# Attention with a mixture of depths on one core: gate products and first ranking later, one transpose per group's sums

## The chip, the core and the metric

The kernel runs on one core of one Trainium2 chip. The core has a matrix engine (TensorE: PE for its matmuls, PEld for its weight loads), a vector engine (VectorE, DVE), an activation engine (ScalarE, ACT), a general engine (GpSimd, POOL), and queues that start DMA transfers; SP is the queue that issues nearly all of them here. Each engine works through its own list of instructions in order, and semaphores tie the lists together. The time of a kernel is the device time of one execution in microseconds (us). The times given are medians over runs; every other number is read from one execution that the hardware profiler recorded.

## The reference

Two blocks follow each other. The first is attention over 8 batches, 12 heads, 448 tokens and head size 64, with root-mean-square normalized queries and keys. The second is a feed-forward net that only the 128 highest scoring tokens of each batch pass through.

```python
def rmsnorm(x, g):
    rms = np.sqrt(np.mean(x * x, axis=-1, keepdims=True) + 1e-06)
    return x / rms * g
q_n, k_n = (rmsnorm(q, g_q), rmsnorm(k, g_k))
scores = scale * np.matmul(q_n, k_n.transpose(0, 1, 3, 2))
scores = scores - np.max(scores, axis=-1, keepdims=True)
attn = np.exp(scores)
attn = attn / (np.sum(attn, axis=-1, keepdims=True) + 1e-09)
x = np.matmul(attn, v)               # then heads side by side: (8, 448, 768)

scores = np.einsum('bsd,d->bs', x, w_gate)
out = x.copy()
for b in range(B):
    top_idx = np.argpartition(-scores[b], capacity)[:capacity]   # 128 of 448
    xe = x[b, top_idx]
    h = np.maximum(xe @ w1, 0.0)     # 768 -> 1024
    ye = h @ w2                      # 1024 -> 768
    g = 1.0 / (1.0 + np.exp(-scores[b, top_idx]))
    out[b, top_idx] = x[b, top_idx] + g[:, None] * ye
```

All data are 32-bit floats.

## The kernel before, in words

**Groups, units, sections.** Four heads make a group; three groups make a batch, 24 groups (n = 0 to 23) in all. A group's 448 keys are cut into seven slices of 64, so that there are 168 units (`u`). The loop at the end of `fast` goes through sections `q` of four units. In a section it issues `scores(u)` (L284, matmuls L292, exponentials L301) for its units and, some units behind, `values(u)` (L309, matmuls L316). What else has to be done is put between them: pieces of the feed-forward net, tasks of a group that ended, and small steps by slot (one slot per unit).

**The sums of the exponentials.** `add_probs` (L324) adds the probabilities of a group's units on the vector engine (L338). For groups 0 to 5, GpSimd adds the first two units (L332) into a buffer called `tok` in the profile, and the vector engine adds that result last (L342); for groups 0 to 5 and 23 the last unit isn't added but becomes a second term. `sum_keys` (L364) sums over keys with matmuls against `pick_pair`, a matrix of ones and zeros (L372): per term four matmuls 224 wide into four different blocks of 32 output rows. A 32-bit matmul is two instructions in the profile, so a term shows as x8. ScalarE copies the result (L380), `invert_sums` (L388) transposes it with two matmuls (L397) and the vector engine takes reciprocals (L399, `rden`). The 448 tokens are four blocks of 112; two of the blocks lie in columns 0 to 111 of the result (`jj` 0) and two in columns 112 to 223 (`jj` 1), and each half takes one of the two transposes.

**From a group to tokens.** `to_tokens(n, c)` (L404) transposes half a group's output (four matmuls L415 into `x_ps`) and the vector engine multiplies it by the reciprocals (L417) into `x`, the batch's tokens.

**Gate and ranking.** `gate(n)` (L433) makes the group's share of the gate scores: four products with a sum each (L441, 112x256, and a short read of the accumulator). After the batch's third group, `spread(b)` (L451) adds the shares, `score_rows` (L463) spreads the scores over partitions with four transposes into `row_ps` (L470), `count` (L480) compares (four times L486), `annotate` (L496) makes five small steps (L501 to L505), `select` (L507) has GpSimd write the chosen rows by four indirect DMAs (L513), and `load_selected` (L529) reads them back through SP (`xe`, L531).

**The feed-forward net.** `mixture(g)` (L538) handles the chosen rows of one batch or of two in pieces: transposes (L561), first layer (L590), second layer (L609), the gated addition (L618), the indirect write to the output (L628). Batch 0 alone is mixture 0: two pieces of transposes, four of the first layer (twelve matmuls 128x128 each) and four of the second (four matmuls 128x384 each). `piece(q)` (L778) issues the next one; there are two places per section for it, and `BEGIN` (L640) and the condition in L781 and L782 say in which sections only the first place is used.

**What sets the order.** `finish` (L694) puts the tasks of a group that ended in a queue, each with the section and place from which it may run; `opening` (L652) runs one of them, with the exception that the inversion may be followed by another. `last_tokens` (L719) puts `gate`, `store_x` and `spread` into slots and `ranks_of` into the queue. `invert_sums` is queued by `sum_keys` (L384 to L386): in the same section if `long_next` (L705) says that a piece of the net follows, and otherwise at the head of the next section. `prepare` (L668) and the lines after it put the squares (L210), their sums (L219), the powers on GpSimd (L220, `rinv`), the broadcast of the norms through memory (`rows` L231, `bc` L242) and the scaling of the queries (L251, `qT`) into slots of the sections before. All this is settled when the program is built: each engine's list is fixed.

**Banks.** The matmul results lie in eight banks: four (`sc`) turn over among scores, and second halves of `x_ps`; two hold the values; one (`aux`) serves `den_ps`, `row_ps` and `x_ps`; one (`moe`) serves the net, and before the net starts it is lent out (`spare`, L125, and the choice in L391 to L395).

Of the kernel before, what the change touches and what calls it, by code (L numbers as in the profile page):

```python
# [10 lines left out]
F32 = mybir.dt.float32  # L11
# [57 lines left out]
def fast(  # L69
# [21 lines left out]
    nc = tc.nc  # L91

    B, NP, _, S = loads.src["qT"].shape
    CP = 112
    NJ = S // CP
    D = 64
    NI = S // D
    H = 2 * NP
    GH = 4
    NG = H // GH  # L100
# [7 lines left out]
    n_groups = B * NG  # L108
    scale = 1.0 / math.sqrt(D)

    const = ctx.enter_context(tc.tile_pool(name="const", bufs=1))
    norm_pool = ctx.enter_context(tc.tile_pool(name="norm", bufs=2))
# [30 lines left out]
    ident = const.tile([128, 128], F32, name="ident")  # L143
# [10 lines left out]

    gg = const.tile([128, 1], F32, name="gg")

    pick_pair = const.tile([128, 32], F32, name="pick_pair")
    nc.vector.memset(pick_pair, 0.0)
    for c in range(2):
        nc.vector.memset(pick_pair[D * c : D * (c + 1), c : c + 1], 1.0)  # L160
    nc.vector.scalar_tensor_tensor(
        out=gg, in0=loads.gcol[:, 0:1], scalar=scale, in1=loads.gcol[:, 1:2], op0=OP.mult, op1=OP.mult
    )

    ps = ps_moe.tile([128, 512], F32, tag="moe", name="warm_ps")
# [116 lines left out]
    probs, sums, avs, xTs, rdens, xs = {}, {}, {}, {}, {}, {}  # L282
# [81 lines left out]
    def sum_keys(n):  # L364

        ps = aux([128, 512], "den_ps")
        terms = [sums.pop(n)] + lasts.pop(n, [])
        for t in terms:
            for hh in range(2):
                for odd in range(2):  # L370
                    o = 64 * odd + 32 * hh
                    nc.tensor.matmul(  # L372
                        out=ps[o : o + 32, 0 : S // 2],
                        lhsT=pick_pair,
                        rhs=t[:, hh].rearrange("k (jj odd p) -> k odd jj p", odd=2, p=CP)[:, odd],
                        start=(t is terms[0]),
                        stop=(t is terms[-1]),
                    )
        den = norm_pool.tile([128, NJ // 2, CP], F32, name="den", bufs=1)
        nc.scalar.copy(out=den.rearrange("d j p -> d (j p)"), in_=ps[:, 0 : S // 2])  # L380
        dens[n] = den
        if n < n_groups - 1:

            q, place = now  # L384
            when = (q, place + 1) if place == 0 or long_next(q) else (q + 1, 0)
            tasks.insert(0, (when, lambda: invert_sums(n)))  # L386

    def invert_sums(n):  # L388
        den = dens.pop(n)
        shape = [128, NJ // 2, 128]  # L390
        if now[1] == 0 and PER * now[0] < units:  # L391
            pool, tag = (ps_moe, "moe") if before_layers(now[0]) else (ps_sc, "sc")
            ps = pool.tile(shape, F32, tag=tag, name="denT_ps")
        else:
            ps = aux(shape, "denT_ps")  # L395
        for jj in range(NJ // 2):
            nc.tensor.transpose(out=ps[:CP, jj, :], in_=den[:, jj, :], identity=ident)  # L397
        rden = norm_pool.tile([CP, NJ // 2, 4, 2], F32, name="rden")
        nc.vector.reciprocal(  # L399
            out=rden, in_=ps[:CP].rearrange("p jj (t r) -> p jj t r", r=32)[:, :, :, 0:2]  # L400
        )
        rdens[n] = rden.rearrange("p jj (odd hh) c -> p (jj odd) hh c", hh=2)

    def to_tokens(n, c):  # L404
        b = n // NG
# [231 lines left out]

    HALVES = 2
    PER = 2 * HALVES
    BEGIN = 3 * NG * NI // PER + 5  # L640
    units = n_groups * NI
    todo, tasks = {}, []

    def at(slot, fn, *args):
        todo.setdefault(slot, []).append(lambda: fn(*args))
# [58 lines left out]

    def long_next(q):  # L705

        if before_layers(q) or q in begin:
            return False
        return 2 <= pieces[0] < pieces[1]

    def before_layers(q):
        return done == 0 and ready.get(0, q + 1) > q
# [6 lines left out]
    def last_tokens(n):  # L719
        to_tokens(n, 1)  # L720
        b, g = divmod(n, NG)
        s = soon()
        at(s, gate, n)
        if g < NG - 1:
            return

        at(s + 4 if s >= 0 else s, store_x, b)
        at(s + 1, spread, b)
        q, place = now

        when = (q + 1 + place // 2, 0) if b < B - 1 else (q + 1, 1)
        tasks.insert(0, (when, lambda: ranks_of(b)))

    def ranks_of(b):
# [39 lines left out]
    def short(q):  # L774

        return pieces[0] == 1

    def piece(q):  # L778

        nonlocal moe, done  # L780
        slow = range(3, 5) if q * PER < units and pieces[1] > 10 else ()  # L781
        if half == 1 and (q in begin and pieces[0] > 2 or pieces[0] in slow):  # L782
            return False
        pieces[0] += 1
        if next(moe, moe) is not moe:
            return True
        if ready.get(done, q + 1) > q:
            return False
        moe = mixture(done)
        pieces[:] = 1, 2 + 8 * len(groups[done])  # L790
        done += 1
        next(moe)
        return True


    begin = range(BEGIN)
    pieces = [0, 0]
    waiting = list(range(units))
    moe, ready, done, q = iter(()), {}, 0, 0
    while done < len(groups) or tasks:  # L800
        now[:] = q, 0
        k = PER * q
# [552 lines left out]
```

## Time and profile before

| what | value |
|---|---|
| median of 3 runs | 523.1 us (522.91 to 523.53) |
| the profiled execution | 523.67 us |
| its span, from the first instruction to the last | 521.9 us |
| PE busy | 499.3 us, 96% of the span |
| VectorE busy | 338.0 us, 65% |
| ScalarE busy | 277.0 us, 53% |
| GpSimd busy | 198.1 us, 38% |
| data moved by DMA | 93.17 MB |

The busy shares are averages over a span with several stages. The kernel starts with loads, squares and scores; from about 102 us pieces of the net lie between the attention's matmuls; after about 447 us only the last group, the last rankings and the net are left. A wait is given as engine, line and what it waited for, with the total in us, the number of waits and the longest. In a timeline, each line has the start and length of a run of equal instructions in us; "[1.60 <-DVE sum L342]" at its end is the engine's idle time ahead of it and what ended that.

### The profile page before, as it was taken

How to read it: one execution, taken by the hardware profiler on the slowest of the kernel's cores; microseconds unless marked ns; L12 is line 12 of the kernel's file. 1: busy time of each engine (PE TensorE's matmuls, PEld its weight loads, DVE VectorE, ACT ScalarE, POOL GpSimd, SP SyncE). 2: the span in 40 equal slices, each digit the busy share in tenths (PEclk: the TensorE clock that was granted, in tenths of full speed). 3: DMA queues.
4: the chain of work that ended last, by engine and by line, in shares of the span. 5: the costliest groups of instructions: out<-in, count | busy, mean ns of one | idle time of the engine just before them, and what ended most of it. 6: DMA issues, size and time to landing. Idle time of an engine off the chain costs nothing. (4 is left out here: it accounts for less than half of the span.)

```text
span 521.9 us, 10414 instructions
## 1 busy us (share of the span) xinstructions
PE 499.3 (96%) x4133; PEld 283.1 (54%) x4133; DVE 338.0 (65%) x636; ACT 277.0 (53%) x507; POOL 198.1 (38%) x110
## 2 busy tenths in 40 slices
PE   5999898899999999999999999999999999899996
PEld 4544343365754534556654454556564464686595
DVE  4578798679867799697656775788464675440101
ACT  4887876666657667675454544764643434310010
POOL 4997768433544084435411344036110132020002
PEclk9999999999999999999999999999999999999999
DMA  8978879989864549968167373586222042031001
GB/s 298 374 239 292 292 242 334 313 233 328 274 177 131 153 142 312 261 229 261 26 201 221 107 240 111 187 264 180 80 76 68 4 148 77 1 122 47 30 32 35
DMA packets 43402, 93.17 MB, mean 179 GB/s; under 512 B 11059, under 2 KB 23348, under 8 KB 43346
## 3 DMA queue, kind: packets, MB, share of 16 engines
q1 hardware_dynamic: 39938, 86.11, 52.6%
q0 software_dynamic: 3264, 6.31, 3.4%
q8 instruction: 34, 0.56, 0.5%
q14 instruction: 22, 0.18, 0.1%
q10 hardware_dynamic: 144, 0.00, 0.0%
HBM read 74.93 MB, written 25.35 MB: 192 GB/s over the span
## 5 line engine op out<-in xcount | busy, mean ns | idle before, releaser
L301 ACT ACTIVATE p<-sc,rinv 128x448 f32<-128x448 f32 x336 | 186.5, 642 | 105.4 <-PE sc L292 79.8
L220 POOL TENSOR_TENSOR rinv<-ss,neg_half 128x14 f32<-128x14 f32 (+1 forms) x49 | 131.3, 2685 | 178.0 <-DVE ss L219 144.9
L292 PE MATMUL sc<-qT,kT 64*64 64x448 f32 x1344 | 153.2, 545 | 2.0 <-DVE x L417 1.2
L316 PE MATMUL av<-p,v 64*64 64x448 f32 x1344 | 146.8, 537 | 0.0
L338 DVE TENSOR_TENSOR sum<-sum,p 128x896 f32<-128x896 f32 x101 | 110.1, 1090 | 8.7 <-ACT p L301 2.5
L316 PEld LDWEIGHTS av<-p,v 64*64 64x64 f32 x1344 | 59.4, 133 | 67.7 <-issue 58.0
L292 PEld LDWEIGHTS sc<-qT,kT 64*64 64x64 f32 x1344 | 54.0, 132 | 70.6 <-issue 46.6
L219 DVE TENSOR_REDUCE ss<-sq 128x14 f32<-128x910 f32 (+1 forms) x49 | 52.4, 1074 | 18.7 <-ACT sq L210 18.5
L417 DVE TENSOR_TENSOR x<-x_ps,rden 112x512 f32<-112x512 f32 x48 | 32.9, 689 | 37.9 <-PE x_ps L415 34.6
L513 POOL DMA_INDIRECT selected<-x,rank x32 | 35.4, 1105 | 58.0 <-DVE x L505 50.0
L590 PE MATMUL moe_ps<-xeT,w 128*128 128x256 f32 (+1 forms) x288 | 56.0, 346 | 0.0
L609 PE MATMUL moe_ps<-w,hT 128*128 128x384 f32 x160 | 55.8, 492 | 0.0
L590 PEld LDWEIGHTS moe_ps<-xeT,w 128*128 128x128 f32 x288 | 46.2, 191 | 7.0 <-issue 2.8
L210 ACT ACTIVATE sq<-tok 128x896 f32<-128x896 f32 (+1 forms) x49 | 46.3, 952 | 6.2 <-DMA tok<-in_tok_dram 6.2
L441 DVE SCALAR_TENSOR_TENSOR prod<-x,wg 112x256 f32<-112x256 f32 x96 | 40.7, 424 | 3.1
L628 POOL DMA_INDIRECT out_dram<-xe,row x10 | 11.4, 1136 | 80.7 <-DVE xe L618 63.6
L609 PEld LDWEIGHTS moe_ps<-w,hT 128*128 128x128 f32 x160 | 28.8, 190 | 20.2 <-issue 4.3
L618 DVE SCALAR_TENSOR_TENSOR xe<-sc,xe 128x384 f32<-128x384 f32 (+1 forms) x7 | 3.9, 560 | 48.1 <-PE sc L609 48.1
L590 PE MATMUL sc<-xeT,w 128*128 128x256 f32 (+1 forms) x192 | 32.2, 328 | 0.3 <-ACT xeT L566 0.3
L609 PE MATMUL sc<-w,hT 128*128 128x384 f32 (+1 forms) x112 | 31.3, 440 | 0.0
L415 PE MATMUL x_ps<-ident,xT 128*112 128x128 f32 x192 | 28.9, 276 | 2.2 <-DVE rden L399 2.2
L590 PEld LDWEIGHTS sc<-xeT,w 128*128 128x128 f32 x192 | 28.8, 191 | 2.9 <-ACT xeT L566 0.5
(69 smaller groups left out, 316.2 us busy)
## 6 DMA issues: line engine op xcount, KB each, us to landing
tok<-in_tok_dram SPq DMA_DIRECT2D x48, 448.0 KB
qT<-in_qT_dram SPq DMA_DIRECT2D x24, 448.0 KB
kT<-in_kT_dram SPq DMA_DIRECT2D x24, 448.0 KB
v<-in_vp_dram SPq DMA_DIRECT2D x24, 448.0 KB
out_dram<-x SPq DMA_DIRECT2D x8, 1344.0 KB
bc<-rows SPq DMA_DIRECT2D x44, 224.0 KB
xe<-selected SPq DMA_DIRECT2D x8, 385.0 KB
w<-in_moe_w_dram SPq DMA_DIRECT2D x6, 512.0 KB
```

The costliest lines, as they stand in the source:

```text
L210: nc.scalar.activation(out=sq[:, h, :, 0:D], in_=t[:, h], func=AF.Square, scale=scale)
L219: nc.vector.tensor_reduce(out=ss[:, h], in_=sq[:, h], axis=AX.X, op=OP.add)
L220: nc.gpsimd.tensor_tensor(out=rinv[:, h].rearrange(flat), in0=ss[:, h].rearrange(flat), in1=neg_half.to_broadcast([128, (h.stop - h.start) ...
L292: nc.tensor.matmul(out=scs[hh][D * c : D * (c + 1), 0:S], lhsT=get("kT", n)[r, c, D * i : D * (i + 1)], rhs=get("qT", n)[r, c, :], start=True,
L301: nc.scalar.activation(out=p[:, hh], in_=scs[hh][:, 0:S], func=AF.Exp, scale=rinvs[n, 1][:, hh, i : i + 1],)
L316: nc.tensor.matmul(out=avs[n][c][D * hh : D * (hh + 1), 0:S], lhsT=get("v", n)[r, hh, i, :], rhs=probs[u][r, hh], start=(i == 0), stop=(i ...
L338: nc.vector.tensor_tensor(out=sums[n], in0=probs.pop(u - 1) if begins else sums[n], in1=probs.pop(u), op=OP.add)
L417: nc.vector.tensor_tensor(out=xs[b][:, :, col : col + 128].rearrange("p j (h d) -> p j h d", d=D), in0=ps[:CP].rearrange("p j (h d) -> p j ...
L441: nc.vector.scalar_tensor_tensor(out=prod, in0=xs[b][:, j, cols], scalar=1.0, in1=wg[:, cols], op0=OP.mult, op1=OP.mult, accum_out=gates[b ...
L513: w = nc.gpsimd.indirect_dma_start(out=t[:, :], out_offset=bass.IndirectOffsetOnAxis(ap=rank[:, j : j + 1], axis=0), in_=x[:, j, :], in_of ...
L590: nc.tensor.matmul(out=ps[:, i, :, :n], lhsT=w1[:, dc, 128 * (f0 + i) : 128 * (f0 + i + 1)], rhs=xeT[:, dc, 0:G, :n], start=(dc == 0), sto ...
L609: nc.tensor.matmul(out=ps[:n, :width], lhsT=hT[:, fc, i, :n], rhs=w2[:, fc, cols], start=(fc == 0), stop=(fc == NFC - 1),)
```

## The change

Four things are changed.

1. **One transpose per group's sums.** `pick_pair` becomes two matrices, one for each half `jj`, whose ones stand in different columns. The halves are then summed into the same 112 columns and different rows: per term eight matmuls 112 wide where there were four 224 wide. The copy of the result is 112 wide and not 224, there is one transpose and not two, and the reciprocal reads the same 16 values per partition in another order and writes them where they were before.
2. **Batch 0's gate products and ranking later.** `gate` of groups 1 and 2 goes two slots later, `spread` of batch 0 too, and `score_rows` of batch 0 may run from place 2 of its section and not place 0. With that, comparison, selection and loading of batch 0's rows move on.
3. **The last gate but one later.** `gate` of group 22 goes four slots later. At the end, that is behind the last addition of group 23's probabilities.
4. **Pieces.** `BEGIN` is 21 and not 20. The condition for using one place per section is put into a function, `single`, and `long_next` asks that function, so that where the second place stays empty, `invert_sums` goes to the head of the next section.

In the lists that are built, besides the parts named, this is what moves: mixture 0 starts one section later (its transposes behind those of group 5 and not group 4), each of its pieces is issued one place later, and the last one fills a place ahead of a `den_ps` that held none; on the vector engine the products of groups 1 and 2 stand behind the additions of groups 2 and 3, batch 0's comparisons behind group 3's reciprocal, and the additions of mixture 0 (L618) later; GpSimd has two powers (`rinv`) ahead of batch 0's selection where it had one ahead and one behind, and, later, batch 2's selection ahead of batch 0's indirect write to the output where it was behind it; SP issues the load of batch 0's rows behind a broadcast and a weight load that stood after it. The lists have as many scores, values, products and pieces as before.

```diff
--- before.py
+++ after.py
@@ -154,10 +154,12 @@
 
     gg = const.tile([128, 1], F32, name="gg")
 
-    pick_pair = const.tile([128, 32], F32, name="pick_pair")
+    pick_pair = const.tile([128, NJ // 2, 32], F32, name="pick_pair")
     nc.vector.memset(pick_pair, 0.0)
-    for c in range(2):
-        nc.vector.memset(pick_pair[D * c : D * (c + 1), c : c + 1], 1.0)
+    for jj in range(NJ // 2):
+        for c in range(2):
+            r = 2 * jj + c
+            nc.vector.memset(pick_pair[D * c : D * (c + 1), jj, r : r + 1], 1.0)
     nc.vector.scalar_tensor_tensor(
         out=gg, in0=loads.gcol[:, 0:1], scalar=scale, in1=loads.gcol[:, 1:2], op0=OP.mult, op1=OP.mult
     )
@@ -365,19 +367,21 @@
 
         ps = aux([128, 512], "den_ps")
         terms = [sums.pop(n)] + lasts.pop(n, [])
-        for t in terms:
+        steps = [(t, jj) for t in terms for jj in range(NJ // 2)]
+        for step in steps:
+            t, jj = step
             for hh in range(2):
                 for odd in range(2):
                     o = 64 * odd + 32 * hh
                     nc.tensor.matmul(
-                        out=ps[o : o + 32, 0 : S // 2],
-                        lhsT=pick_pair,
-                        rhs=t[:, hh].rearrange("k (jj odd p) -> k odd jj p", odd=2, p=CP)[:, odd],
-                        start=(t is terms[0]),
-                        stop=(t is terms[-1]),
+                        out=ps[o : o + 32, 0:CP],
+                        lhsT=pick_pair[:, jj],
+                        rhs=t[:, hh].rearrange("k (j p) -> k j p", p=CP)[:, 2 * jj + odd],
+                        start=(step is steps[0]),
+                        stop=(step is steps[-1]),
                     )
-        den = norm_pool.tile([128, NJ // 2, CP], F32, name="den", bufs=1)
-        nc.scalar.copy(out=den.rearrange("d j p -> d (j p)"), in_=ps[:, 0 : S // 2])
+        den = norm_pool.tile([128, CP], F32, name="den", bufs=1)
+        nc.scalar.copy(out=den, in_=ps[:, 0:CP])
         dens[n] = den
         if n < n_groups - 1:
 
@@ -387,19 +391,21 @@
 
     def invert_sums(n):
         den = dens.pop(n)
-        shape = [128, NJ // 2, 128]
+        shape = [128, 128]
         if now[1] == 0 and PER * now[0] < units:
             pool, tag = (ps_moe, "moe") if before_layers(now[0]) else (ps_sc, "sc")
             ps = pool.tile(shape, F32, tag=tag, name="denT_ps")
         else:
             ps = aux(shape, "denT_ps")
-        for jj in range(NJ // 2):
-            nc.tensor.transpose(out=ps[:CP, jj, :], in_=den[:, jj, :], identity=ident)
-        rden = norm_pool.tile([CP, NJ // 2, 4, 2], F32, name="rden")
+        nc.tensor.transpose(out=ps[:CP, :], in_=den, identity=ident)
+        rden = norm_pool.tile([CP, NJ // 2, 2, 2, 2], F32, name="rden")
         nc.vector.reciprocal(
-            out=rden, in_=ps[:CP].rearrange("p jj (t r) -> p jj t r", r=32)[:, :, :, 0:2]
+            out=rden.rearrange("p jj odd hh c -> p (odd hh) jj c"),
+            in_=ps[:CP].rearrange("p (t r) -> p t r", r=32)[:, :, 0:NJ].rearrange(
+                "p t (jj c) -> p t jj c", c=2
+            ),
         )
-        rdens[n] = rden.rearrange("p jj (odd hh) c -> p (jj odd) hh c", hh=2)
+        rdens[n] = rden.rearrange("p jj odd hh c -> p (jj odd) hh c")
 
     def to_tokens(n, c):
         b = n // NG
@@ -637,7 +643,7 @@
 
     HALVES = 2
     PER = 2 * HALVES
-    BEGIN = 3 * NG * NI // PER + 5
+    BEGIN = 3 * NG * NI // PER + 6
     units = n_groups * NI
     todo, tasks = {}, []
 
@@ -704,7 +710,7 @@
 
     def long_next(q):
 
-        if before_layers(q) or q in begin:
+        if before_layers(q) or single(q):
             return False
         return 2 <= pieces[0] < pieces[1]
 
@@ -720,15 +726,16 @@
         to_tokens(n, 1)
         b, g = divmod(n, NG)
         s = soon()
-        at(s, gate, n)
+        late = 2 if n in (1, NG - 1) else 4 if n == n_groups - 2 else 0
+        at(s + late, gate, n)
         if g < NG - 1:
             return
 
         at(s + 4 if s >= 0 else s, store_x, b)
-        at(s + 1, spread, b)
+        at(s + 1 + late, spread, b)
         q, place = now
 
-        when = (q + 1 + place // 2, 0) if b < B - 1 else (q + 1, 1)
+        when = (q + 1 + place // 2, late) if b < B - 1 else (q + 1, 1)
         tasks.insert(0, (when, lambda: ranks_of(b)))
 
     def ranks_of(b):
@@ -775,11 +782,16 @@
 
         return pieces[0] == 1
 
+    def single(q):
+
+        if q in begin:
+            return pieces[0] > 2
+        return PER * q < units and pieces[1] > 10 and pieces[0] in (3, 4)
+
     def piece(q):
 
         nonlocal moe, done
-        slow = range(3, 5) if q * PER < units and pieces[1] > 10 else ()
-        if half == 1 and (q in begin and pieces[0] > 2 or pieces[0] in slow):
+        if half == 1 and single(q):
             return False
         pieces[0] += 1
         if next(moe, moe) is not moe:
```

## The prediction

> **What bounds the kernel now.** I read the busy shares first, then PE's waits, then the timeline of PE and of the vector engine around each wait. PE is busy 96% of the span, so two things can shorten the kernel: less PE work, or fewer of the waits that make up the rest.
>
> ```profile
> PE 499.3 (96%) x4133; PEld 283.1 (54%) x4133; DVE 338.0 (65%) x636; ACT 277.0 (53%) x507; POOL 198.1 (38%) x110
> ...
> PE den_ps L372 <- DVE sum L342: 2.7, 2, 1.6
> PE x_ps L415 <- DVE rden L399: 2.2, 1, 2.2
> PE moe_ps L561 <- DMA xe<-selected: 2.2, 1, 2.2
> PE den_ps L372 <- DVE row L573: 1.3, 1, 1.3
> PE sc L292 <- DVE x L417: 1.2, 1, 1.2
> PE den_ps L372 <- DVE sum L338: 1.0, 1, 1.0
> PE denT_ps L397 <- ACT den L380: 1.0, 2, 0.5
> ```
>
> These seven lines are 11.6 us, nearly all of PE's waiting after its start. Next, PE's timeline where they lie.
>
> ```profile
> 57.13 0.58 PE L372 MATMUL den_ps<-sum,pick_pair 128*32 128x224 f32 x8 [1.60 <-DVE sum L342]
> ...
> 74.44 0.58 PE L372 MATMUL den_ps<-sum,pick_pair 128*32 128x224 f32 x8 [1.05 <-DVE sum L342]
> ...
> 84.57 0.65 PE L415 MATMUL x_ps<-ident,xT 128*112 128x128 f32 x4 [2.19 <-DVE rden L399]
> ...
> 101.82 0.55 PE L561 MATMUL moe_ps<-ident,xe 128*128 128x128 f32 x3 [2.17 <-DMA xe<-selected]
> ...
> 110.14 0.43 PE L397 MATMUL denT_ps<-ident,den 128*112 128x128 f32 x2
> 110.40 0.60 PE L415 MATMUL x_ps<-ident,xT 128*112 128x128 f32 x4
> 110.84 2.84 PE L590 MATMUL moe_ps<-xeT,w 128*128 128x128 f32 x24
> ```
>
> Three of the first four waits end with the vector engine, whose own list shows what stands in front (a group of four products is 68.19 to 70.06).
>
> ```profile
> 71.59 2.80 DVE L342 TENSOR_TENSOR sum<-sum,tok 128x896 f32<-128x896 f32 x1
> ...
> 89.13 1.15 DVE L251 SCALAR_TENSOR_TENSOR qT<-qT,gg,bc 128x896 f32<-128x896 f32 x1 [0.34 <-DMA bc<-rows]
> ...
> 99.52 0.25 DVE L399 RECIPROCAL rden<-denT_ps 112x16 f32<-112x16 f32 x1
> ```
>
> The first took 2.80 us where its kind takes 1.09. The second shows the vector engine waiting for the broadcast of the norms: a limit that no reordering of sums removes.
>
> **The change, part by part.** The sum is made against the profiled execution, 523.67 us, which is 0.6 above the median of 523.1.
>
> *One transpose instead of two.* Two `denT_ps` matmuls take 110.14 to 110.40, 0.26 from start to next start; four `x_ps` take 0.44. One transpose is thus 0.109 on PE, 24 are removed. Four of them (groups 2 to 5) are inside the stretch worked below, so 20 count here: -2.2. The copy of `den` (0.34 us at 224 wide) gets shorter on ScalarE, beside PE's work; I count nothing for it.
>
> *Eight matmuls 112 wide instead of four 224 wide,* 31 terms. A term costs 0.38 now: two passes of four different column blocks, 0.189 each, the four starting 7 ns apart. If a pass goes by its width, four passes of half the width cost the same 0.38. The nearest rows of small matmuls (`sc` L262, 64x64, 26 ns from start to start) would make 16 instructions 0.42, so 1.2 us in all. A gain is excluded as long as the columns streamed are the same. I take +0.1, nearer the width since the row of the same operation shows the four overlapping, and keep +1.2. The added memsets at the start are under 0.15 and lie in the same term.
>
> The Trainium skill, "TensorE: Matmul & The Clock Gate", section "Wait — 56ns, not 53.3ns?", says that starts never come closer than about 25 ns. The rows contradict it for matmuls in different column blocks (7 ns). By the page a term would be an estimated 0.40 and this part about +0.7 us.
>
> *The early stretch, 55 to 115 us* (gate products and ranking later, net a section later). I replay the lists:
> - `den_ps` of group 2 no longer stands behind 1.87 us of products; its sum is ready at 55.2, so the 1.60 wait goes. But ScalarE is busy without pause from 54.2 to 61.5, and GpSimd's `tok` addition of 65.90 to 67.96 still frees the probabilities' buffers: at 67.7 little of this is left.
> - `den_ps` of group 3: products, gate steps and `row_ps` (0.39) are no longer in front. It comes at 72.2 to 72.8 and not 74.44, and `denT_ps` at 79.15, not 81.51.
> - Comparisons (4 x 0.76) now lie behind group 3's reciprocal, so the 2.19 wait goes. `den_ps` of group 4 at 87, not 91.72.
> - Now a new wait. The vector engine still gets the broadcast at 89.03 and then has, in its list, `qT` 1.1, products 1.9, two `ss` 2.1, sums 4.4 and the reciprocal 0.25: 98.75, against 99.77 before. The second half of group 4's tokens sits in the net's lent bank and needs that reciprocal; PE arrives at 94.6 and waits some 4.3 us. Most of what was gained goes back.
> - `den_ps` of group 5 at 99.7 and not 103.06; the reciprocal of group 5 at 107.1 and not 110.60; the next scores at 108.45 and not 114.05. That is -5.6, but one piece of the first layer (2.68) has not been done yet. Net -2.9, and -0.2 of transposes before it would be double, so I take -2.8.
> - The load of the chosen rows: selection on GpSimd ends about 91 (87.66 before), the rows are in memory 6 us later, the load then takes 5.5 to 8.4 (93.40 to 101.78 before): 103 to 106. PE asks for them at 107.2. No wait, with 1 to 4 us to spare.
>
> Behind the later steps: the products of groups 1 and 2 stand behind two additions, and only the batch's ranking needs them. On SP the load passes behind one broadcast and one weight load (0.6 MB together), which land earlier for it; GpSimd's second `rinv` (2.6) goes ahead of the selection.
>
> The 2.80 against 1.09 of the sum above lies over GpSimd's `tok` addition, which took 2.92 at 70.51 where its kind takes 2.09: each held the other up. A rule speaks against this move: the Trainium skill, "SBUF — State Buffer", section "Who interferes with whom", says that a vector instruction with two SBUF inputs contends with a GpSimd instruction that reads SBUF, and that one of them blocks for the whole of it. Products have both inputs in SBUF, as that sum has. By the page, an estimated 2.09 us of the gain would go if group 2's products, now two slots later, meet that addition; by my replay they come behind it and nothing goes.
>
> *Between, 123 to 178.* The net's pieces come a place later each; PE is busy for 55.0 of 55 us there, so their order costs it nothing while each piece finds its data, which the vector engine's and ScalarE's 77% and 63% leave room for. The gated addition (0.6) and batch 0's write to the output move with the net, batch 2's selection ahead of that write on GpSimd; the write ends in memory that nothing reads, and GpSimd is busy 39% there. If this cover were gone, a late piece would hold PE for its reader's wait, 0.3 to 1 us as at L566 and L397.
>
> *The middle, 178 to 204.* The vector engine has no pause from 177.9 to 208, and PE waits at 191.52 and 203.16: 1.21 and 1.36 us from the end of the work ahead. The net's last piece (2.58) now stands ahead of the first of them and does the work in that time: -2.6. It is the piece not done in the early stretch, so the sum of PE's work is unchanged. Bounds: 0, if the vector list comes later by the piece, and -2.6.
>
> *Two short waits of `denT_ps`* (231.76 and 349.28, 0.49 and 0.47). The inversion now goes behind the next scores: -1.0. Nothing is late for it: the reciprocal's reader stands behind those scores as well.
>
> *The tail.* At 450.18 the last `den_ps` waits 1.35 behind four products (447.28 to 449.04) and a sum. With the products behind the sum: -1.4. Then the last gate is ready about 457, and `row_ps` comes on PE at 459: no new wait.
>
> *Sum:* -2.2 + 0.1 - 2.8 - 2.6 - 1.0 - 1.4 = -9.9. 523.67 - 9.9 = 513.8 by the profiled execution; 0.6 less for the median, 513.2.
>
> **The rivals.**
> *A: as worked.* 50%; own range 512 to 516.
> *B: the vector engine keeps the pace.* The wait at 94.6 grows by 2.8, because the vector engine is held up over a `tok` addition (1.7 each time, 2.80 less 1.09) or the broadcast lands later, and the early gain goes; in the middle the vector list has as much to do as before and gives none of the 2.6. For it: no pause there from 177.9 to 208. Against: the waits there are only as long as the piece. 513.2 + 5.4 = 518.6; with +1.2 for the terms, 519.8. 24%.
> *C: the new wait isn't there.* The broadcast, whose rows are computed on GpSimd, lands earlier too, and none of the four early waits has a successor. They are 1.60 + 1.05 + 2.19 + 2.17 = 7.0, against the 2.8 taken: 4.2 better, 509.0. Against it: SP's queue is full then. 10%.
> *D: slower, by the chosen rows.* `row_ps` to rows took 29.0 us (72.80 to 101.78). From `row_ps` at 79.3 that makes 108.3, against 107.2 asked for: 1.1 lost. Each us beyond is one for one on PE, since the net's transposes stand in its list ahead of the attention. The kernel gets slower once the rows land later than about 117. For it: a load behind the others and DMA's share at 0.8 to 0.9 there; against: nothing in the trace took 10 us longer. 9%.
> *E: no difference,* gains and new waits cancel: 7%.
>
> **How the numbers follow.** Time is that of A. From 509.5 to 520 lie A and B with the bounds of the terms, and the part of C where one of its waits keeps a successor; the rest of C, D and E are about 2 in 10. About 0.2% (1.05 us) is what a measurement of this kernel can tell from none. Faster is A, B and C, 84%; within it 7%; slower 9%.
>
> **What the profile after would show.** `denT_ps` x1 and PE's busy time lower by 2 to 3; `den_ps` terms of 16 instructions 0.38 apart (0.42 would mean the issue bounds them). No wait at `den_ps` of groups 2 and 3; a wait of `x_ps` on `rden` near 95 to 99, some 4 us, which is the step I trust least. No wait at L561. At 178 to 204 no wait above 0.3, and none of `denT_ps` on ScalarE. What would make it wrong: that wait larger than 5, a wait of L561 on the load, or scores waiting for ScalarE where they did not.

## The result and the profile after

In the runs by which the prediction is measured, the changed kernel takes 522.6 us (520.22 to 524.43, 14 runs) and the kernel before 522.63 us (14 runs): a ratio of 1.0003, 95% interval 0.9986 to 1.002. That is no difference, where 9.9 us less was forecast. Three later sets of the same program, each beside the kernel before on its chip, are shown under the experiments: 519.6, 518.9 and 519.6 us, 2.5 to 3.7 us less than before. So two questions stand: why the change brings some 3 us and not 10, and why the first set shows not even these.

The first line is from the page of the changed kernel (first set), the next from its answer on PE's waits (engine, line, what was waited for; us in total, number, longest).

```profile
PE 504.6 (97%) x4357; PEld 288.5 (55%) x4357; DVE 340.6 (65%) x638; ACT 274.9 (53%) x507; POOL 198.2 (38%) x110
```

```profile
PE x_ps L421 <- DVE rden L402: 3.5, 2, 3.1
PE sc L294 <- DVE x L423: 0.9, 1, 0.9
...
PE sc L294 <- ACT p L303: 0.6, 1, 0.6
```

Every wait in the list of before is gone or small, those on the sums, on the chosen rows and on ScalarE's copy among them. One is new, the wait of `x_ps` on `rden`. But PE's busy time went up, from 499.3 to 504.6, with less work: some of its work ran slower or was held up. PE's timeline shows where (start, length, the run of instructions; idle time ahead of it).

```profile
55.72 0.59 PE L376 MATMUL den_ps<-sum,pick_pair 128*32 128x112 f32 x16
...
73.03 0.59 PE L376 MATMUL den_ps<-sum,pick_pair 128*32 128x112 f32 x16
...
101.91 0.65 PE L421 MATMUL x_ps<-ident,xT 128*112 128x128 f32 x4 [3.10 <-DVE rden L402]
102.71 0.90 PE L376 MATMUL den_ps<-sum,pick_pair 128*32 128x112 f32 x16
103.36 0.99 PE L376 MATMUL den_ps<-p,pick_pair 128*32 128x112 f32 x16
```

`den_ps` of groups 2 and 3 wait for nothing, as worked. After the wait at 101.91, a `den_ps` run of 0.59 takes 0.90 to 0.99. The table by stretches (us; busy time of PE, its weight loads, VectorE, ScalarE and GpSimd; granted clock; share and rate of the DMA engines) has the reason in its clock column:

```profile
98.00:102.00 4.00, 0.90 (x9) 0.60 (x7) 3.65 (x6) 1.82 (x3) 3.74 (x2) 1.00 0.80 251
102.00:104.00 2.00, 1.85 (x36) 1.56 (x36) 1.93 (x5) 0.00 (x0) 0.00 (x0) 0.71 1.02 317
104.00:106.00 2.00, 2.00 (x20) 0.71 (x16) 1.93 (x7) 0.25 (x1) 0.00 (x0) 0.50 1.00 364
106.00:108.00 2.00, 2.00 (x28) 0.72 (x24) 1.89 (x3) 1.85 (x4) 0.00 (x0) 0.94 1.05 414
```

After the idle time the granted clock falls to one half, from 102.85 to 106.26: 3.41 us, of which half, 1.7 us, is lost.

What the wait is made of stands in the timelines of VectorE and GpSimd.

```profile
91.35 2.86 DVE L447 SCALAR_TENSOR_TENSOR prod<-x,wg 112x256 f32<-112x256 f32 x1
```

```profile
91.82 2.10 POOL L334 TENSOR_TENSOR tok<-p 128x896 f32<-128x896 f32 x1
```

A product of group 3, 0.42 us elsewhere, takes 2.86: it begins just ahead of GpSimd's `tok` addition for group 5 and ends 0.3 after it. The reciprocal that PE waits for stands behind it. (This is so in the first three sets; the profile of the fourth has another cause ahead of that reciprocal, shown under the experiments.)

To see where the time goes, I take the start of each group's `den_ps` and subtract the start of the same group's in the profile of before (us; negative is earlier). From group 6 to 9, a kernel whose net begins later has one piece (2.68 us) still to do, which it does ahead of group 10's.

| `den_ps` of group | 2 | 4 | 5 | 6 | 9 | 11 | 12 | 13 | 18 | 19 | 22 | 23 |
|---|---|---|---|---|---|---|---|---|---|---|---|---|
| changed kernel, first set | -1.4 | -2.8 | -0.4 | -0.3 | -0.5 | +3.0 | +2.9 | +2.1 | +1.6 | +0.9 | +0.6 | -0.9 |
| changed kernel, third set | -1.5 | -2.9 | -0.7 | -0.7 | -1.1 | -0.8 | -0.9 | -1.7 | -2.2 | -3.0 | -3.2 | -4.7 |
| without the second part | +0.1 | +1.3 | -1.2 | -1.3 | -1.8 | -1.9 | -2.0 | -2.8 | -3.3 | -4.0 | -4.3 | -5.8 |
| first part alone | -0.1 | -0.1 | -0.7 | -0.8 | -1.4 | -1.5 | -1.6 | -1.8 | -2.3 | -2.5 | -2.7 | -2.8 |
| changed, no `tok` addition for group 5 | -1.5 | -2.9 | -3.6 | -3.8 | -4.2 | -3.9 | -4.1 | -4.9 | -5.3 | -6.1 | -6.4 | -7.9 |
| the same, and group 3's products later | -2.0 | -3.4 | -6.1 | -6.7 | -7.1 | -6.8 | -6.9 | -7.8 | -8.3 | -9.0 | -9.3 | -10.8 |

The profile of before is of an execution 1 us above its median, so a row's last number is larger than the difference of medians. The steps in a row are what counts. The lower rows are explained below.

### The profile page after: what moved, and what is told of

The parts are those of the page before. It is cut to its first block, busy times and chain, and to the rows that moved or that the text cites. A ratio compares the mean times of both kernels' runs of the same rounds, so it can differ in the third digit from the quotient of the medians.

```text
span 520.9 us, 10869 instructions
## 1 busy us (share of the span) xinstructions
PE 504.6 (97%) x4357; PEld 288.5 (55%) x4357; DVE 340.6 (65%) x638; ACT 274.9 (53%) x507; POOL 198.2 (38%) x110
## 5 line engine op out<-in xcount | busy, mean ns | idle before, releaser
L222 POOL TENSOR_TENSOR rinv<-ss,neg_half 128x14 f32<-128x14 f32 (+1 forms) x49 | 133.7, 2733 | 178.8 <-DVE ss L221 152.4
L294 PE MATMUL sc<-qT,kT 64*64 64x448 f32 x1344 | 159.6, 549 | 2.4 <-DVE x L423 0.9
L318 PE MATMUL av<-p,v 64*64 64x448 f32 x1344 | 151.2, 537 | 0.2 <-issue 0.2
L340 DVE TENSOR_TENSOR sum<-sum,p 128x896 f32<-128x896 f32 x101 | 112.9, 1118 | 8.6 <-ACT p L303 2.4
L318 PEld LDWEIGHTS av<-p,v 64*64 64x64 f32 x1344 | 60.8, 133 | 68.3 <-issue 58.0
L519 POOL DMA_INDIRECT selected<-x,rank x32 | 34.3, 1071 | 56.4 <-DVE x L511 48.6
L447 DVE SCALAR_TENSOR_TENSOR prod<-x,wg 112x256 f32<-112x256 f32 x96 | 45.0, 468 | 3.0
```

The costliest lines, as they stand in the source:

```text
L222: nc.gpsimd.tensor_tensor(out=rinv[:, h].rearrange(flat), in0=ss[:, h].rearrange(flat), in1=neg_half.to_broadcast([128, (h.stop - h.start) ...
L294: nc.tensor.matmul(out=scs[hh][D * c : D * (c + 1), 0:S], lhsT=get("kT", n)[r, c, D * i : D * (i + 1)], rhs=get("qT", n)[r, c, :], start=True,
L318: nc.tensor.matmul(out=avs[n][c][D * hh : D * (hh + 1), 0:S], lhsT=get("v", n)[r, hh, i, :], rhs=probs[u][r, hh], start=(i == 0), stop=(i ...
L340: nc.vector.tensor_tensor(out=sums[n], in0=probs.pop(u - 1) if begins else sums[n], in1=probs.pop(u), op=OP.add)
L447: nc.vector.scalar_tensor_tensor(out=prod, in0=xs[b][:, j, cols], scalar=1.0, in1=wg[:, cols], op0=OP.mult, op1=OP.mult, accum_out=gates[b ...
L519: w = nc.gpsimd.indirect_dma_start(out=t[:, :], out_offset=bass.IndirectOffsetOnAxis(ap=rank[:, j : j + 1], axis=0), in_=x[:, j, :], in_of ...
```

## The experiments

The theory: the second part (batch 0's products and ranking) makes a new wait of PE, through a product that is held up over a GpSimd addition, and the wait brings a stretch of half clock; the other parts give what was worked. The rivals: the parts give nothing by themselves; or the vector engine's list, or the net's later start, makes the loss in any arrangement. Each set has the kernel before on the same chip: medians 522.16, 522.58, 522.47 and 522.76.

### The changed kernel again, three times

> The changed kernel once more, beside the others on the same chip. Theory (the new wait): no difference from the kernel before, some 522.6 us, a wait of the second x_ps of group 4 on rden of about 3 us near 99 to 102, and the granted clock at one half for about 3.4 us behind it. Rival (the changed kernel is paced elsewhere, for instance by the idle of ScalarE at 191 to 197): the same stops of ScalarE come again at the same places, and PE's loss between group 10's and group 11's den_ps is again some 2 us. If that stop is gone here, it was of one execution alone.

> The changed kernel a third time, beside the next three on one chip. Two sets of runs gave 522.6 (no difference) and 519.6 (2.5 us less than before), at about equal granted clocks; the profile of the first has a stop of ScalarE at 191 to 196.7 us that costs PE some 2.4 to 3.3 us, the second has none. Theory (the stop belongs to that set of runs, not to the change): 519 to 520.5 and no such stop. Rival (it is of the kernel and comes and goes from run to run): a time between, with runs in two groups some 3 us apart at the same clock.

> The changed kernel a fourth time. Theory (the first set was the odd one): 518.5 to 520, ScalarE's copy of group 10's den within 0.1 us of its sum on PE, the clock at half for 3.4 or 6.8 us behind the wait near 102 us. Rival (the program has two courses that come about equally): 522 to 523, with a stop of ScalarE of 3 us or more near 191 to 197 us in the profile.

Measured: 519.64 (ratio 0.9956, interval 0.9939 to 0.9972), 518.93 (0.994, 0.992 to 0.996) and 519.63 (0.9927, 0.9898 to 0.9955). The wait of `x_ps` on `rden` was there each time, 4.0, 3.6 and 4.5 us long, with the clock at half for 6.8, 3.4 and 6.8 us.

What stands behind the wait isn't the same each time. In the second and third sets a product of group 3 is held up again (2.31 and 2.84 us). In the fourth, which has the longest wait, none is:

```profile
92.17 1.61 DVE L253 SCALAR_TENSOR_TENSOR qT<-qT,gg,bc 128x896 f32<-128x896 f32 x1 [3.04 <-DMA bc<-rows]
93.70 0.41 DVE L447 SCALAR_TENSOR_TENSOR prod<-x,wg 112x256 f32<-112x256 f32 x1
```

```profile
102.29 1.10 PE L421 MATMUL x_ps<-ident,xT 128*112 128x128 f32 x4 [4.48 <-DVE rden L402]
```

VectorE stands idle for 3.04 us until the broadcast of the norms has landed; most of the `tok` addition (90.73 to 92.82) lies over that idle time, and only the scaling of the queries is lengthened, by 0.46. So a late broadcast alone makes the wait as long as the hold-up does. In the other profiles of the changed kernel and its variants that scaling starts between 88.7 and 91.2; why the broadcast lands so differently from execution to execution is open.

As to the time, the first set is the odd one, by some 3 us. Its profile differs between groups 10 and 11, where it loses 2.1 us and the third set gains 1.0. There ScalarE stands still:

```profile
196.73 0.25 ACT L384 COPY den<-den_ps 128x112 f32<-128x112 f32 x1 [5.71 <-PE av L318]
```

In the profile of the fourth set, as in the second and third, it comes 2.1 us after the instruction before it, as `den_ps` allows:

```profile
193.74 0.25 ACT L384 COPY den<-den_ps 128x112 f32<-128x112 f32 x1 [2.08 <-PE den_ps L376]
```

The sum on PE began at 192.42 in the first set and took its usual 0.59, so for 3.7 us nothing that the profile records held ScalarE. Its runs lie 3 us above those of the later sets at the same mean clock (522.25 and 522.57 against 517.85 to 519.68, all at 0.995), so the stop, or something like it, was in most of them. A shorter one of the same kind stands at 92.39, where that copy comes 2.4 us behind its sum. What they are is open; no other profile has them.

### Without the second part

> The changed kernel without its second part: batch 0's gate products, spreading and ranking stand where they were, and the net begins a section earlier as before. What is left is one transpose for two, the products of group 22 behind the last sum, and the inversion behind the next scores. Theory (the second part makes a wait that eats the gain of the others): 24 x 0.109 of transposes, 1.0 of the two short waits, 1.4 at the end, less 0.4 at the start: 4.6 us less than before, some 518.0. Rival (the other parts give nothing on the whole, because eight matmuls a term or the start cost as much as the transposes give): 521.5 to 523.

```diff
-    BEGIN = 3 * NG * NI // PER + 6
+    BEGIN = 3 * NG * NI // PER + 5
-        late = 2 if n in (1, NG - 1) else 4 if n == n_groups - 2 else 0
+        late = 4 if n == n_groups - 2 else 0
```

Measured: 517.27, ratio 0.9899 (0.9878 to 0.9919), 4.9 us less than before; 4.6 was expected. On that chip the changed kernel took 519.64. The three other parts thus give what was worked, and the second part, forecast at 5.4 gained, costs 2.4. In part the agreement is luck: this kernel's profile has a half clock of its own (3.4 us from 85.29, 1.7 lost), and the wait for the chosen rows, 2.2 in the profile of before, is not in it.

### The first part alone

> The kernel before with the first part alone: one transpose for two, eight matmuls 112 wide a term. Theory: PE's work is less by 24 x 0.109 = 2.6, terms cost the same (0.38 from term to term), the memsets cost 0.4 at the start; what lies in stretches where PE waits anyway (four groups) gives nothing: 1.8 us less than before, 520.8. Rival (starts no closer than some 25 ns): terms 0.42 apart, 31 x 0.04 = 1.2 less of a gain, 522.

```diff
-        if before_layers(q) or single(q):
+        if before_layers(q) or q in begin:
-        late = 2 if n in (1, NG - 1) else 4 if n == n_groups - 2 else 0
+        late = 0
```

(`BEGIN` goes back to 20 as well.) Measured: 520.45, ratio 0.9959 (0.9943 to 0.9975), 1.7 less. In PE's timeline of this kernel, a term after a term:

```profile
41.64 0.59 PE L376 MATMUL den_ps<-sum,pick_pair 128*32 128x112 f32 x16 [0.22 <-DVE x L423]
42.05 0.57 PE L376 MATMUL den_ps<-p,pick_pair 128*32 128x112 f32 x16
42.55 1.74 PE L294 MATMUL sc<-qT,kT 64*64 64x448 f32 x16
```

The starts are 0.41 and 0.50 apart; before, 41.61, 42.01 and 42.51, they were 0.40 and 0.50. Sixteen instructions of half the width cost 0.01 more than eight, 0.3 us in all 31 terms at most. The floor that the prediction cites from the Trainium skill, "TensorE: Matmul & The Clock Gate", section "Wait — 56ns, not 53.3ns?" (25 ns between starts, 0.40 a term and 0.7 us by the estimate made of it), can't be told from this.

### The products of group 3 later

> The changed kernel, and the gate products of group 3 six slots later, so that they stand on the vector engine behind group 4's reciprocal and both its token halves, with the products of group 4. Nothing else moves. Theory (the vector engine's list in front of that reciprocal makes PE's wait of 3.1 us, and the wait makes 3.4 us of half clock, 1.7 us more): no wait of x_ps on rden above 0.5 us, clock 0.998 or more, 522.6 - 4.8 = 517.8 us. Rival (the second half of group 4's tokens comes late for PE's own scores and values, and the products only fill the time): the wait stays above 2 us and the time within 1 us of the changed kernel's.

```diff
-        at(s + late, gate, n)
+        at(s + (6 if n == NG else late), gate, n)
```

Measured: 516.23, ratio 0.988 (0.9853 to 0.9907), 3.4 less than the changed kernel on that chip. A part of the theory fell: the wait was not gone, it was 2.7 us. With the products out of the way, another instruction met GpSimd's addition, as the timelines of this kernel's VectorE and GpSimd show:

```profile
90.30 3.55 DVE L253 SCALAR_TENSOR_TENSOR qT<-qT,gg,bc 128x896 f32<-128x896 f32 x1 [1.09 <-DMA bc<-rows]
```

```profile
90.80 2.08 POOL L334 TENSOR_TENSOR tok<-p 128x896 f32<-128x896 f32 x1
```

The scaling of the queries (1.15 us elsewhere) has two inputs in SBUF like a product, and ends 1.0 after the addition. So it is the addition that matters, whichever instruction with two such inputs it meets.

### Without GpSimd's addition for group 5, and the same in the kernel before

> The changed kernel, with the vector engine adding all of group 5's units: GpSimd's tok addition for that group, at 91 to 93 us, is gone, one sum of 1.09 is added on the vector engine. Theory (a product, 0.42 us, is held up for the length of that tok addition and takes 2.3 to 2.9, all of it ahead of group 4's reciprocal): the product takes 0.42, the reciprocal comes 1 to 3 us earlier since the added sum falls into the vector engine's idle time before x, PE's wait of x_ps on rden falls from 4.0 to 1 to 3, and the clock's half window behind it becomes rarer: 2 to 4 us less than the changed kernel. Rival (the vector engine's list is as long in any case and the broadcast of the norms sets it): wait and time within 1 us of the changed kernel's.

```diff
     def by_pool(n):
-        return n < 2 * NG
+        return n < 2 * NG - 1
```

Measured: 514.10, ratio 0.9834 (0.9815 to 0.9853). The changed kernel on that chip took 518.93: 4.8 less, by one addition that goes from GpSimd to VectorE. In this kernel's timeline of VectorE the product is as short as any other, and in that of PE the wait is 2.0:

```profile
91.75 0.42 DVE L447 SCALAR_TENSOR_TENSOR prod<-x,wg 112x256 f32<-112x256 f32 x1
...
98.38 0.25 DVE L402 RECIPROCAL rden<-denT_ps 112x16 f32<-112x16 f32 x1
```

```profile
98.69 0.79 PE L421 MATMUL x_ps<-ident,xT 128*112 128x128 f32 x4 [1.99 <-DVE rden L402]
```

The reciprocal is 2.9 us earlier than in the third set (101.31): 2.4 of hold-up is gone, and two sums now fill time in which VectorE waited for `x_ps` (idle 2.95, now 0.77). The rest of the 4.8 is the clock: the mean over the runs is 0.998 where the changed kernel has 0.994, and 0.4% of 518 is 2.1 us.

> The kernel before, with the vector engine adding all of group 5's units (no tok addition on GpSimd for it, one sum of 1.09 more). In the profile of before that addition, 90.30 to 92.39, lies over vector instructions with one input in memory and over idle time, and nothing is held up. Theory (the tok addition cost the changed kernel 4.8 only because the second part puts products over it): no difference from before, 521.5 to 523. Rival (the addition on GpSimd is a loss in any arrangement, and dropping it is worth some 4 us by itself): 518 or less.

Measured: 522.79, ratio 1.0011 (0.9994 to 1.0028). By the medians of 12 and 17 runs, the same edit in the kernel before (the edit above, in its `by_pool`) changes nothing. (Its profile is of its fastest execution, 520.81, and lacks the 2.2 us wait of before for the chosen rows.) The addition is a loss only where the second part puts instructions with two inputs over it. That decides against the rival for which it is a loss anywhere.

### Both, and group 4 too

> The changed kernel without group 5's tok addition (514.1) and with the products of group 3 behind group 4's reciprocal. Theory: the wait of x_ps on rden that is left, 2.0 us, was 1.9 of products in front of that reciprocal, so it goes down to under 0.5, and the half clock of 3.4 us that followed it in the profile (1.7 us) doesn't come: clock 0.998 or more, 514.1 - 1.9 - up to 1 (where the half clock came) = 511.5 to 512.5. Rival (the reciprocal is bound by something behind the products): the wait stays above 1.5, and 513.5 to 514.5.

> The version without group 5's tok addition and with group 3's products behind group 4's reciprocal, beside the changed kernel on one chip. Theory: 513.4 again, 5.5 to 6.5 less than the changed kernel. Rival (its gain was of that chip): 515 or more.

The two edits together: `by_pool` as above, and group 3's products six slots later. Measured: 513.38 (0.9835, 0.9808 to 0.9862) and, on another chip beside the changed kernel's 519.63, 512.96 (0.9796, 0.9762 to 0.9831). PE's waits in the first of these (`warm_ps` at the very start left out):

```profile
PE sc L294 <- DVE qT L273: 0.8, 1, 0.8
PE sc L294 <- DVE row L579: 0.7, 1, 0.7
PE sc L294 <- ACT p L303: 0.6, 1, 0.6
PE den_ps L376 <- DVE x L423: 0.4, 2, 0.2
PE sc L264 <- POOL rinv L222: 0.4, 1, 0.4
PE x_ps L421 <- DVE rden L402: 0.4, 1, 0.4
```

No wait above 0.8, no half clock before the end in either profile, and the best time of all, 9.1 to 9.8 less than before. It is a little above the 511.5 to 512.5 expected.

> The one before, with group 4's units on the vector engine as well: its tok addition, 71 to 73 us, over which a product of group 2 takes 2.3 and not 0.42. Theory: 1.9 us of hold-up goes and a sum of 1.09 comes; nothing of it is in front of what PE waits for (group 4's den_ps comes late for its second x_ps, which comes late for PE's own work), so 0 to 0.5 us less than the one before. Rival (this hold-up costs as the other does): 1.5 us less or more.

> The changed kernel with both tok additions (groups 4 and 5) on the vector engine, products of group 3 where the change has them. Theory: as with group 5's alone, 513.5 to 514.5, with PE's wait of x_ps on rden near 2 us. Rival (group 4's costs too): 512.5 or less.

The same two kernels with `return n < 2 * NG - 2`. Measured: 513.42 (0.9843, 0.9813 to 0.9873), the same as without this edit, and 515.28 (0.9864, 0.9826 to 0.9903), where 514.10 stood without it on another chip; the intervals overlap, but 513.5 to 514.5 was expected, and a wait near 2 us. The wait was 3.1, with half clock behind it and no product held up: the broadcast came late here too (VectorE idle for 1.73 ahead of the scaling, which starts at 91.20). The first of the two comparisons was made on one chip, with the broadcast on time in both profiles. By it the hold-up at group 4's addition, where a product of group 2 took 2.3 (2.30 at 71.67 in the first set), costs nothing that can be measured: PE isn't waiting for what comes behind it.

### What of the second part gains and what loses

> The changed kernel without its second part, as in the run without batch 0's move (517.3), but with the products of group 1 alone two slots later, behind group 2's last addition. Theory (ScalarE and GpSimd's buffers keep the pace after group 2, as the replay had it): the 1.6 wait of group 2's den_ps goes, little of it is left at group 4: 0 to 0.6 less, 516.7 to 517.3. Rival (the gain stays, as the changed kernel's own den_ps of group 2 to 4 say, 1.9 to 3.2 us earlier): 515.5 or less.

```diff
-    BEGIN = 3 * NG * NI // PER + 6
+    BEGIN = 3 * NG * NI // PER + 5
-        late = 2 if n in (1, NG - 1) else 4 if n == n_groups - 2 else 0
+        late = 2 if n == 1 else 4 if n == n_groups - 2 else 0
```

Measured: 518.45, ratio 0.9927 (0.9909 to 0.9945), against 0.9899 without the edit: no gain, if anything a small loss. Group 2's `den_ps` comes 1.7 us earlier than in the profile of before, group 3's only 0.4, for PE then waits 0.6 for ScalarE's exponentials and 0.7 for the sum. The replay had this right.

> The changed kernel with batch 0's products, spreading and ranking where they were before, but with the net a section later all the same: only the moment from which mixture 0 may run is put back by a section. Theory (the loss of the second part comes from the vector engine's list and the ranking's place, and the net's later begin is a gain: the last piece fills the waits at 190 to 204, and the wait for the chosen rows goes): 2.3 and up to 1.7 less than the 517.3 of the run without the second part, 513.3 to 515. Rival (the later net itself makes the loss, because the lent bank makes the second x_ps of group 4 wait for its reciprocal): 517 to 520, with a wait of x_ps on rden of 3 us or more.

```diff
-        late = 2 if n in (1, NG - 1) else 4 if n == n_groups - 2 else 0
+        late = 4 if n == n_groups - 2 else 0
-            ready[group_of[b]] = (s + 8) // PER + 1
+            ready[group_of[b]] = (s + 8) // PER + 1 + (b == 0)
```

Measured: 516.12, ratio 0.9883 (0.9864 to 0.9903); 4.9 us less than before without the later net, 6.5 with it. From group 9 to group 11 this kernel does a piece of 2.58 in 0.3 us more than before does without it: 2.3 gained at that place, as in the changed kernel's later sets. The lent bank costs 0.5 (a wait of `x_ps` at 99.85), not 3. So the rival that blamed the net's later start falls. That it is a gain on the whole is not shown by the times: the ratios 0.9883 and 0.9899 are from two chips and their intervals overlap. The time is 1 us above the 513.3 to 515 expected; why is open.

## Why the prediction was wrong

**The first, third and fourth parts** were right, and so was their sum. Worked were 2.6 for all 24 transposes, 1.0 for the short waits and 1.4 at the end, 5.0 in all; the kernel that has only these gained 4.9. In the third set's row the step from group 12 to 13 is -0.8 and from 18 to 19 -0.8, which with a transpose taken off each is 1.4, a little more than the 1.0; the step from 22 to 23 is -1.5, of which 0.1 is a transpose. The terms cost 0.01 more each, 0.3 at most in all: more than the +0.1 taken, well inside the bound of 1.2. The last `row_ps` found the last gate ready: it starts at 459.62, and the gate is written by 457.4.

**The middle** was right where the first set's stop of ScalarE is absent: 2.3 of the 2.6; 0.3 of the wait of scores on `x` stays. (The two waits there, read as 1.21 and 1.36, are 1.05 and 1.20 in PE's timeline of before.)

**The early stretch** was wrong, and the step that failed is the fourth of the replay: "qT 1.1, products 1.9, two ss 2.1, sums 4.4 and the reciprocal 0.25: 98.75". The new wait was foreseen at its place, with 4.3 us of length and its cause (VectorE's list ahead of the reciprocal), but four terms in it were off.
- The products took 4.3 in the first set, 3.7 and 4.2 in the next two, and not 1.9. The hold-up by GpSimd was weighed, with the Trainium skill, "SBUF — State Buffer", section "Who interferes with whom", and the row of 2.80 against 1.09, but only for group 2's products and group 4's addition, and then set to nothing. Both of those did meet (2.30 at 71.67) without cost. The pair that counts, group 3's products and group 5's addition, was not looked at: the replay gave start times for PE and VectorE there, but none for GpSimd behind the selection, which ended at 91.8 in the first set. In every profile in which such a pair met, the vector instruction was lengthened, as that rule says.
- The broadcast was taken to land at 89.03 as before. It set the scaling's start at 90.03 in the second set and at 92.17 in the fourth, where the products took 1.8 and the reciprocal came latest of all. How often this second cause acts, no run here tells.
- PE came to the second `x_ps` at 97.5 to 98.8, not at 94.6, so the wait was no longer than foreseen (3.1 to 4.5) while it ended later, at 101.6 to 102.3 and not 98.9. Of this, 1.3 to 2.0 us were there at group 4's `den_ps` already (88.3 to 89.0, not 87). In the later sets, scores between the two waited 0.5 to 1.4 for ScalarE's exponentials, and these for the buffers that the same `tok` addition frees (1.60 of ScalarE's idle time ends with it in the third set).
- The wait has a price behind its end, the half clock. No term of the sum has it. In the profile of before, with no wait above 2.2 us after the start, there is none, so the trace of before did not show it; in the profiles of the changed kernel it comes every time.

At group 6 the replay had -5.6 (with a piece less done); the third set has -0.7. Of the 4.9 between them, 2.8 are the later reciprocal (done at 101.56 and not 98.75) and 1.7 the half clock; 0.4 is not accounted for. The kernel without hold-up and wait gets 513.0 to 513.4, the number that was predicted; that is no support for the sum, which had a wait of 4.3 us in it. Rival B had the mechanism ("held up over a `tok` addition") and a time of 518.6; of it the early half was right, and the middle was not lost. That its time is so near the 518.9 to 519.6 of the later sets is luck: it has a loss of 2.6 in the middle that didn't come, and lacks the half clock that did.

The rows landed in time (at 104.5 in the second set and 106.5 in the fourth; PE asks for them at 112.0 in the first, and in none of the four profiles waits), so D did not come into play.

## What to carry to other kernels

When work moves on one engine's list, set the new times against the instructions of every engine that was seen to hold it up, one by one, and not only at the place that one thought of: here one addition of 2.1 us on GpSimd decided over 4.8 us in the set that compared them. A wait that is moved is not of the same price at its new place: a half clock can follow it, so bring PE's longest idle time down first. Take a transfer's landing as a range and not as one number when an instruction waits for it. And a replay that puts a new wait of 4 us on the critical engine is a reason to change the order further: two lines more turned 3 us of gain into 9.

## What the runs showed of the hardware

- The half clock comes in windows. It lasted 3.41 or 6.83 us behind the wait in all four profiles of the changed kernel (waits of 3.1 to 4.5 us) and 3.41 in the one without group 4's and 5's additions (3.1). Behind shorter waits it came sometimes: after 2.3 us in the run without the second part and in the one with group 1's products later, and after 2.0 in the one without group 5's addition; not after 2.7 in the one with group 3's products later, nor after the 2.3 of the first part alone and of the later net.
- The Trainium skill, "TensorE: Matmul & The Clock Gate", section "What's actually happening", says that the clock goes to half after an idle window of about 3.4 us, and that the windows run free. The traces agree with the windows: from the rise of the clock near the start to its fall there are 92.16 us in five profiles, 88.75 in a sixth and 75.09 in two more, which is 27, 26 and 22 times 3.413. They do not agree with a window that must be wholly idle. Cut the span at these steps and add up PE's idle time in each window at full clock, away from the start and the end: half clock followed all seven windows with 1.99 to 2.84 us of idle time, one of the two with 1.86, and none with 1.72 or less. So about 2 us in one window is enough here. A window already at half clock, with 1.64 or 1.73 of idle time, was followed by a second one; these are the two cases of 6.83. The wait of 2.7 was cut in two by a step, with 1.7 and 1.2 of idle time in the two windows, and had no half clock behind it. By an estimate from these numbers, a wait of 4 us or more brings the half clock wherever it lies, and the 4.3 us of the replay thus had a further price of at least 1.7.
- Over all sets the mean granted clock is 0.997 for the kernel before and 0.994 for the changed one, 0.998 to 0.999 for the version without the wait. 0.3% of 518 is 1.6 us, half as much as the changed kernel gains in the later sets. (Single runs of the kernel before lie between 0.994 and 1.000, so the half clock comes there too in some executions, though not in the profiled one before its end.)
- One set of runs of a program can lie 3 us from three others of the same program, while the kernel beside it stays within 0.6. A comparison of two kernels by one set has that much more uncertainty than its interval says.
